# Strassen sums kept in PSUM, more of the second weight on chip, and an instruction order read from a table

## The chip, the core and the metric

The kernel runs on one NeuronCore of a Trainium2 chip. The metric is the device time of one execution in microseconds (us), from the first to the last instruction and what lies around them. TensorE (PE) multiplies matrices, VectorE (DVE) and ScalarE (ACT) work element by element, GpSimd (POOL) takes element work that needs no PSUM, and SyncE (SP) issues nearly all transfers, in order, from one queue.

## What is computed

The reference is linear attention with random features over 8 batches of 8 heads (576 tokens, 64 features per head), followed by a two-layer network over all 4608 tokens. Everything is float32.

```
q, k scaled by 64 ** -0.25
phi(x) = exp(x @ omega.T - |x|^2 / 2 - max) / sqrt(128)
attn   = (phi(q) @ (phi(k).T @ v)) / (phi(q) @ sum(phi(k)) + 1e-6)
x      = attn as [4608 tokens, 512]
h      = x @ w_in                     # 512 -> 2048
g      = h where h > 0, else exp(min(h, 0)) - 1
out    = g @ w_out                    # 2048 -> 512
```

The two weights arrive as 64-bit floats and are turned into float32 on the chip.

## The kernel before, in words

**Precision.** A float32 matmul operand is split into a high part and a low part (what is left), both in the fast matmul format, and a product is three passes: low times high, high times high, high times low. The helper at L433 to L440 makes the parts: `copy` the high one (on ACT or DVE), `tt` the low one (on POOL or DVE).

**Tiling.** The 4608 tokens are nine blocks of 512 (`TB`). The 2048 hidden features are 16 steps `f` of 128. `layer1` (L1234) makes one step of the first layer for blocks 0 and 1 with ordinary matmuls. For blocks 2 to 8, `quad` (L1281) makes two steps, a pair, with one level of Strassen's scheme: seven products in place of eight, each of 128 by 256 columns and six matmuls, into two PSUM banks pa and pb. Both write the activated tiles g, and `layer2` (L1359) multiplies a step's g by that step's part of w2 and adds it into the four banks `acc` of the block: twelve matmuls of 512 columns a step. PSUM has eight banks: four hold `acc`, the other four are shared by the pairs and by the attention (one tag, `pa`).

**The sums of Strassen's scheme.** On the side of x they are made by `operands` (L994): x lies in a ring `xf` for two blocks (L425), four sums S1 to S4 go to buffers of their own (tag `u`, L1005), and the seven operands are split into high and low. On the side of w1 `combine` (L1187) makes them once, and eight slots per pair lie in DRAM (`w1p`). `weights` (L1141) fetches, for each pair of a block, four tiles: slots 1 and 2, 3 and 4, 7, and 5 and 6 (L1178 to L1183). On the side of the result, `quad` copies the first half of pa to `s` (ACT, L1319), adds on DVE out of PSUM into an SBUF buffer `h` (L1314), and runs the activation out of `h` and pa: relu and exp on ACT (L1333, L1342), the rest on DVE (L1347), in pieces of 256 and 512 columns.

**The second weight.** Its parts 0 to 7 stay on chip (`w2h`, `w2l`, L419 and L420; `NRES` = 8). Parts 8 to 15 are written to DRAM once (`w2s`) and fetched by SP for every block (L1154) into two buffers (tag `w2`), 512 KB each.

**Stages.** Attention of batch b is worked in the segment before its tokens are needed; its projections, exponentials, sums and divisions lie between the matmuls of the network. Blocks 0 and 1 run in two halves of eight steps each, since the weights are being converted at the same time (`from_f64`, L1051). Attention ends before block 7, so blocks 7 and 8 have only the network.

**Order.** Each piece of work is a task with an engine, a duration, a due time and what it reads and writes (`Plan.op`, L149). `Plan.order` (L175) runs an event loop over estimated durations and emits, for each engine, the ready task that is due first; some tasks may go to a second engine (`other`, L354). Due times come from constants at the head (`STEP`, `OFF1`, `QOFF`, `LAGQ`, ...). Engines and queues run in the order emitted. Buffers are named by a tag, and `SLOTS` (L78) tells how many each tag has; a task that needs a buffer waits for the last reader of the one whose place it takes.

```python
SLOTS = {'raw': 3, 'u': 5, 'h': 5, 'ld': 2, 't': 2, 'e': 3, 'w1': 5, 'g': 3, 'w2': 2, 'xo': 8}
products(q[0], pa, ((0, 0, "A11", True), (1, 1, "S2", False)), wq[0])
products(q[1], pb, ((0, 0, "S3", True), (1, 1, "S1", False)), wq[1])
products(q[2], pa, ((0, 0, "A12", False),), wq[2])
products(q[3], pb, ((0, 0, "A22", False), (1, 1, "S4", False)), wq[3])
```

Of the kernel before, what the change touches and what calls it, by code (L numbers as in the profile page):

```python
# [19 lines left out]
P = 128  # L20
# [13 lines left out]
RING = 2 * TB  # L34
# [14 lines left out]
MLP0 = 23.44  # L49
SEG = [7.276, 7.148, 5.642, 7.92]  # L50
STEP = 6.384
STEP_ATT = 6.65

LAG = 2.608


PAIR0 = 24.011
DUE_LOAD, DUE_K, DUE_KV, DUE_Q = 19.218, 25.325, 28.271, 24.877
LOAD2, K2, KV2, Q2 = 7.188, 37.601, 24.27, 26.068
TAIL = 7.114  # L60
TAIL2 = 4.433
HEAD = 24.713


CONV1 = 27.076
CONV_STEP = -0.248
CONV2 = 2.044

EARLY = 22.132
CONV3 = 60.74  # L70
# [6 lines left out]
NRES = 8  # L77
SLOTS = {'raw': 3, 'u': 5, 'h': 5, 'ld': 2, 't': 2, 'e': 3, 'w1': 5, 'g': 3, 'w2': 2, 'xo': 8}  # L78

OPERANDS = ("A11", "S2", "S3", "S1", "A12", "A22", "S4")  # L80

# [6 lines left out]
DUE_Z = 15.231  # L88
# [3 lines left out]
EARLIER = 8.077  # L92
# [19 lines left out]

class Buf:
# [13 lines left out]
class Plan:  # L127
# [3 lines left out]

    LAT = {
        "PE": dict(PE=0, ACT=220, DVE=205, POOL=270, SP=300),
        "ACT": dict(PE=500, ACT=200, DVE=155, POOL=280, SP=300),
        "DVE": dict(PE=480, ACT=150, DVE=127, POOL=215, SP=300),
        "POOL": dict(PE=400, ACT=100, DVE=100, POOL=102, SP=300),
        "SP": dict(PE=400, ACT=200, DVE=200, POOL=200, SP=200),
    }
    LOOSE = ("pa", "h")

    SHARED = ("DVE", "POOL")

    FREE = dict(PE=1100.0, ACT=730.0, DVE=1600.0, POOL=1300.0, SP=700.0)
    DMA_LAT, DMA_RATE = 1050.0, 300.0
# [30 lines left out]
    def order(self):  # L175
        tasks = self.tasks
        waits = [len(t[3]) for t in tasks]
        users = [[] for _ in tasks]
        for n, t in enumerate(tasks):
            for d in t[3]:  # L180
                users[d].append(n)
        ready = [dict.fromkeys(t[0], t[7] * 1e3) for t in tasks]
        end = [0.0] * len(tasks)
        free, queue, events = {}, {}, [0.0]
        held = dict.fromkeys(self.SHARED, 0.0)
        kind = 0
        slots, dma = {}, 0.0


        line = {}  # L190
        for n in sorted(range(len(tasks)), key=lambda n: tasks[n][1]):
            for b in sorted(tasks[n][4], key=lambda b: b.args[3]):
                q = line.setdefault(b.key, [])
                if not b.listed:
                    b.listed = True
                    q.append(b)
                    slots.setdefault(b.key, [0.0] * b.n)
        for q in line.values():
            q.reverse()
        for n, t in enumerate(tasks):  # L200
            for e in t[0]:
                free.setdefault(e, self.FREE[e])
                heapq.heappush(events, self.FREE[e])
                queue.setdefault(e, [])
                if not waits[n]:
                    queue[e].append(n)
                    heapq.heappush(events, ready[n][e])
        done, last = [], {}
        now = 0.0

        events = sorted(set(events))

        def mine(n, eng):

            engs, due = tasks[n][:2]
            end = now + engs[eng][0] + engs[eng][1] * 1e3
            for e, (ns, late) in engs.items():
                if e == eng:
                    continue
                t = max(free[e], now, ready[n][e])  # L220
                if e == "POOL":
                    t = max(t, held["DVE"])
                elif e == "DVE" and tasks[n][6]:
                    t = max(t, held["POOL"])
                t += ns + late * 1e3
                for m in queue[e]:
                    if m != n and tasks[m][1] < due and len(tasks[m][0]) == 1:
                        t += tasks[m][0][e][0]
                        if t >= end:
                            break  # L230
                if t < end:
                    return False
            return True

        while len(done) < len(tasks):
            started = False
            for eng, q in queue.items():
                if free[eng] > now:
                    continue
                best, first = None, 0.0  # L240
                for n in q:
                    engs, due, _, _, bufs, _, port, _, full = tasks[n]
                    if eng == "PE" and full == kind:
                        due -= STICK
                    if ready[n][eng] > now:
                        continue
                    if best is not None and due >= first:
                        continue
                    if eng == "DVE" and port and held["POOL"] > now or eng == "POOL" and held["DVE"] > now:
                        continue  # L250
                    if len(engs) > 1 and not mine(n, eng):
                        continue
                    need = {}
                    for b in bufs:
                        if b.slot is None:
                            need.setdefault(b.key, []).append(b)
                    for key, bs in sorted(need.items()):
                        s = sum(z <= now for z in slots[key])
                        head = line[key][-1]
                        if s < len(bs):  # L260
                            for b in bs:
                                b.waits = True
                            break
                        if head not in bs and (s < 2 or key not in self.LOOSE or head.waits):
                            break
                    else:
                        best, first = n, due
                if best is None:
                    continue
                started = True  # L270
                engs, _, _, _, bufs, nbytes, port, _, full = tasks[best]
                for e in engs:
                    queue[e].remove(best)
                ns = engs[eng][0]
                if eng == "PE":
                    ns += SWITCH if kind and not full else 0.0
                    kind = full
                for b in bufs:
                    if b.slot is None:
                        s = slots[b.key]  # L280
                        b.slot = s.pop(s.index(min(s)))
                        line[b.key].remove(b)
                free[eng] = now + ns
                if eng == "POOL" or eng == "DVE" and port:
                    held[eng] = now + ns
                    if now < YIELD:
                        self.behind[best] = last.get("DVE") if eng == "POOL" else None
                    last[eng] = best
                if nbytes:
                    dma = max(now + self.DMA_LAT, dma) + nbytes / self.DMA_RATE  # L290
                    end[best] = dma + self.DMA_LAT + self.lands[best]
                else:
                    end[best] = now + ns
                heapq.heappush(events, free[eng])
                done.append((best, eng))
                for b in bufs:
                    b.left -= 1
                    if not b.left:
                        heapq.heappush(events, end[best] + 200.0)
                        slots[b.key].append(end[best] + 200.0)  # L300
                for u in users[best]:
                    for e in ready[u]:
                        ready[u][e] = max(ready[u][e], end[best] + self.LAT[eng][e])
                    waits[u] -= 1
                    if not waits[u]:
                        for e in ready[u]:
                            queue[e].append(u)
                            heapq.heappush(events, ready[u][e])
            if not started:
                if not events:  # L310
                    raise RuntimeError("no task can start")
                now = max(now, heapq.heappop(events))
        return done

    def issue(self, tc):
# [4 lines left out]
        for n, eng in order:  # L320
# [10 lines left out]
YIELD = 2e6  # L331
STICK = 3.202
SWITCH = 90.0
ENGINES = dict(DVE=mybir.EngineType.DVE, POOL=mybir.EngineType.Pool)
# [41 lines left out]
def performer_elu_kernel(  # L376
# [764 lines left out]
    def weights(F, due):  # L1141
# [29 lines left out]
        elif blk < NCONV:  # L1171
            op("SP", 590, due - 8, lambda: nc.sync.dma_start(raw_of(t), both), parts, keys, P * 3440)
            if odd:
                combine(j, w1c[F - 1], t, due + TJOB)
# [401 lines left out]
```

## Time and profile before

| what | us |
|---|---|
| median of 3 runs | 1028.62 |
| lowest, highest | 1023.39, 1030.73 |
| the profiled execution's own time | 1025.38 |
| its span, first to last instruction | 1023.1 |

The profile is one execution. Busy time of an engine is the time in which it has an instruction under way. Matmuls overlap (a new one starts before the last has drained), so the duration of one is longer than the distance to the next. A granted clock of 1.00 is 2.4 GHz, one of 0.50 is 1.2 GHz.

### The profile page before, as it was taken

The page shows a single profiled execution, that of the slowest core. Times are in us where ns is not written, and L with a number is a line of the kernel's source. Part 1 is how long each engine was busy: PE and PEld are TensorE (multiplying, and loading weights), DVE is VectorE, ACT ScalarE, POOL GpSimd, SP SyncE. Part 2 cuts the span into 40 slices and gives each one's busy share as a digit, 9 for nine tenths or more (in the row PEclk, how much of TensorE's full clock was granted, in tenths as well). Part 3 has the DMA queues.
Part 4 walks back from the last instruction along what each step waited for, and adds up shares of the span by engine and source line. Part 5 has one row for each costly group of instructions (what it writes and reads, how often), then busy time and mean ns, then how long its engine had stood idle before and what let it go on. Part 6 is the DMA issues. An engine that isn't in the chain of part 4 may idle for free.

```text
span 1023.1 us, 20461 instructions
## 1 busy us (share of the span) xinstructions
PE 984.9 (96%) x6237; PEld 848.9 (83%) x6237; DVE 791.8 (77%) x2775; ACT 693.2 (68%) x1886; POOL 411.0 (40%) x398
## 2 busy tenths in 40 slices
PE   7999998899988999999999999999999989999998
PEld 7888777678767988899889988898899869899996
DVE  6999788767889997999898988898899545364331
ACT  6898656788678786788688778787878534243231
POOL 2555744585424544154424432443345412222322
PEclk9999999999997999999999999999999999999999
DMA  8687768789998989799979888998898679568654
GB/s 214 181 250 246 261 252 303 264 289 313 317 315 320 309 265 285 265 336 283 282 266 353 273 272 269 326 292 281 282 320 272 186 226 317 187 210 284 216 175 144
DMA packets 104523, 273.70 MB, mean 268 GB/s; under 512 B 13216, under 2 KB 26336, under 8 KB 104416
## 3 DMA queue, kind: packets, MB, share of 16 engines
q1 hardware_dynamic: 103472, 270.09, 81.3%
q10 hardware_dynamic: 944, 2.33, 0.7%
q8 instruction: 50, 0.82, 0.3%
q14 instruction: 57, 0.47, 0.2%
HBM read 225.71 MB, written 46.66 MB: 266 GB/s over the span
## 4 chain that ended last, share of the span: by engine, by line
PE 68%; DMA 11%; DVE 10%; ACT 6%; issue 2%; POOL 2%; SPq 0%; POOLq 0%; ACTq 0%; DVEq 0%
PE acc L1375 32%; PE phb L1300 14%; PE pha L1300 11%; DMA w<-w2s 6%; PE ppk L631 2%; PE ppq L631 2%; DVE junk L851 1%; ACT hk L532 1%; DMA xk<-in_kx_dram 1%; PE pn L767 1%; DMA w1q<-w1p 1%; PE ph L1249 1%; ACT hq L532 1%; DVE u_w L1103 1%; PE ph L1251 1%
## 5 line engine op out<-in xcount | busy, mean ns | idle before, releaser
L440 POOL TENSOR_TENSOR g<-e,g 128x512 fp32r<-128x512 f32 x128 | 166.2, 1299 | 370.0 <-DVE g L437 106.1
L1375 PE MATMUL acc<-w,g 128*128 128x512 f32 x861 | 224.8, 399 | 12.1 <-DMA w<-w2s 9.5
L1375 PEld LDWEIGHTS acc<-w,g 128*128 128x128 f32 x861 | 155.5, 190 | 44.0 <-DMA w<-w2s 9.7
L1375 PE MATMUL acc<-w2h,g 128*128 128x512 f32 x576 | 185.6, 395 | 0.0
L1375 PEld LDWEIGHTS acc<-w2h,g 128*128 128x128 f32 x576 | 106.3, 189 | 19.5 <-issue 0.5
L1375 PE MATMUL acc<-w2l,g 128*128 128x512 f32 x288 | 114.4, 397 | 2.2 <-DVE g L437 1.9
L1333 ACT ACTIVATE e<-h 128x256 f32<-128x256 f32 x112 | 58.7, 525 | 78.9 <-DVE h L1314 77.2
L440 POOL TENSOR_TENSOR hq<-hq,den 128x512 f32<-128x512 f32 (+1 forms) x96 | 78.2, 833 | 62.0 <-DVE den L860 45.4
L437 DVE CAST g<-e 128x512 fp32r<-128x512 f32 x128 | 58.4, 461 | 48.5 <-PE acc L1375 47.0
L640 ACT ACTIVATE p2q<-ppq,sqq 128x128 f32<-128x128 f32 x216 | 65.4, 367 | 21.5 <-PE ppq L631 18.7
L851 DVE CUSTOM_DVE_ANT_0 junk<-hq,pz 128x128 f32<-128x128 f32 (+1 forms) x320 | 73.1, 280 | 6.8 <-PE pz L830 5.9
L640 ACT ACTIVATE p2k<-ppk,sqk 128x128 f32<-128x128 f32 x216 | 66.1, 370 | 15.9 <-PE ppk L631 14.2
L1333 ACT ACTIVATE e<-pha 128x256 f32<-128x256 f32 x56 | 21.5, 385 | 73.9 <-PE pha L1300 73.7
L532 ACT ACTIVATE hk<-hk,mnk 128x128 f32<-128x128 f32 x216 | 69.1, 403 | 2.3 <-DVE mnk L649 2.0
L532 ACT ACTIVATE hq<-hq,mnq 128x128 f32<-128x128 f32 x216 | 68.7, 398 | 1.3 <-DVE mnq L649 1.0
L649 DVE CUSTOM_DVE_ANT_0 hq<-ppq,p2q 128x128 f32<-128x128 f32 x216 | 53.1, 285 | 20.4 <-ACT p2q L640 19.2
L1342 ACT ACTIVATE e<-e 128x512 f32<-128x512 f32 x112 | 65.7, 629 | 0.8
L1375 PEld LDWEIGHTS acc<-w2l,g 128*128 128x128 f32 x288 | 54.3, 189 | 12.1 <-DVE g L437 2.1
L1347 DVE SCALAR_TENSOR_TENSOR e<-e,h 128x256 f32<-128x256 f32 (+1 forms) x112 | 61.3, 584 | 1.4 <-ACT e L1342 1.4
L649 DVE CUSTOM_DVE_ANT_0 hk<-ppk,p2k 128x128 f32<-128x128 f32 x216 | 53.1, 283 | 11.8 <-ACT p2k L640 11.0
L1249 PE MATMUL ph<-xc,w1c 128*128 128x512 f32 x128 | 53.4, 418 | 3.9 <-DVE e L1262 1.6
L1314 DVE TENSOR_TENSOR h<-phb,h 128x512 f32<-128x512 f32 x56 | 38.6, 690 | 21.2 <-PE phb L1300 20.4
(223 smaller groups left out, 2398.2 us busy)
## 6 DMA issues: line engine op xcount, KB each, us to landing
w1q<-w1p SPq DMA_DIRECT2D x168, 512.0 KB, 5.5
w<-w2s SPq DMA_DIRECT2D x72, 512.0 KB, 5.5
raw_w<-in_w_dram SPq DMA_DIRECT2D x28, 512.0 KB, 4.7
w1q<-w1p SPq DMA_DIRECT2D x56, 256.0 KB, 4.9
xk<-in_kx_dram SPq DMA_DIRECT2D x24, 576.0 KB, 6.0
xq<-in_qx_dram SPq DMA_DIRECT2D x24, 576.0 KB, 6.5
turned<-tb SPq DMA_DIRECT2D x48, 288.0 KB, 5.7
qh<-turned SPq DMA_DIRECT2D x96, 144.0 KB, 7.1
```

The lines of the kernel that those rows point to most:

```text
L437: nc.vector.tensor_copy(dst, src)
L440: (nc.vector if e == "DVE" else nc.gpsimd).tensor_tensor(*args)
L532: nc.scalar.activation(h()[:, j, :], src(j), AF.Exp, bias=mn()[:, j:j + 1], scale=-1.0)
L640: nc.scalar.activation(p2()[:, a], view()[:, a, M:], AF.Identity, bias=sq()[:, j:j + 1], scale=1.0)
L649: nc.vector.tensor_tensor_reduce(out=h()[:, j, :], in0=view()[:, a, 0:M], in1=p2()[:, a, :], scale=1.0, scalar=HIGHEST, op0=ALU.add, op1=A ...
L851: nc.vector.tensor_tensor_reduce(out=junk()[r], in0=h()[r, j, :], in1=pz()[r, a * P:(a + 1) * P], scale=1.0, scalar=EPS, op0=ALU.mult, op1 ...
L1249: nc.tensor.matmul(ph(), wh, x[:, 0], start=(c == 0), stop=False)
L1300: nc.tensor.matmul(half(p, n), a, b, start=(first and c == 0 and i == 0), stop=(c == 1 and i == 2), skip_group_check=True)
L1333: op("ACT", act(n, psum), d, lambda: nc.scalar.activation(out(), x(), AF.Relu, scale=-1.0), reads, writes)
L1342: "ACT", act(TB), d + 0.6 + 0.2 * n, lambda z=z: nc.scalar.activation(e()[:, z], e()[:, z], AF.Exp, scale=-1.0), keys, keys,
L1347: "DVE", dve(n), d, lambda: nc.vector.scalar_tensor_tensor(out(), out(), -1.0, x(), ALU.add, ALU.max), (*reads, *keys), keys,
L1375: nc.tensor.matmul(now[tt](), g()[:, a, ts], w(), start=(first and n == 0), stop=(last and n == 2))
```

## The change

- In `quad` the buffers `h` and `e` of four parts are gone. The sums are added in place: into `s`, into the second half of pa, and into pb. Relu, exp and the rest then run on whole banks of 512 columns, reading PSUM. A g tile now holds half of the tokens of both steps of the pair, so `layer2` of either step reads both tiles.
- `operands` makes the four sums in the buffers of x itself (new tiles `xf`, two per block, four slots) after the parts that need the old contents are split.
- 12 of 16 parts of w2 stay on chip, in one tile `w2r` with high and low side by side. Parts 3, 7, 11 and 15 are fetched, into one buffer.
- The last two loads of w1 of a pair become one of three slots, 768 KB, into one buffer of its own (tag `w1b`); it serves the products A12, A22 and S4.
- The slots per tag change, tag `e` goes, and in the last three pairs of block 8 the g tiles lie in the buffers of tag `h`.
- `Plan.order` no longer plans: it reads `ORDER`, a list of 5098 numbers, each four times a task's number plus the place of the engine chosen. The constants change too, but with the table they set no order.

```diff
-NRES = 8
-SLOTS = {'raw': 3, 'u': 5, 'h': 5, 'ld': 2, 't': 2, 'e': 3, 'w1': 5, 'g': 3, 'w2': 2, 'xo': 8}
+STREAMED = (3, 7, 11, 15)
+SLOTS = {'raw': 3, 'u': 8, 'h': 5, 'ld': 2, 't': 2, 'w1': 3, 'w1b': 1, 'g': 2, 'w2': 1, 'xo': 7, 'xf': 4}
+
+def xc_tag(blk, c):
+    return "w1b" if (blk, c) == (NCONV - 1, NC - 1) else "xo"
...
+ORDER = """
+0 44 52 48 8 12 56 36 77 40 4 276 142 66 72 96 297 280 301 1004 108 100 112 144 148 68 172 176 80 84 288 152 16 104 20 284 60 500 88 24 1140 496 1008
...
     def order(self):
...
+        done, last = [], None
+        for x in map(int, ORDER.split()):
+            n, e = divmod(x, 4)
+            eng = list(self.tasks[n][0])[e]
+            if eng == "POOL":
+                self.behind[n] = last
+            elif eng == "DVE" and self.tasks[n][6]:
+                last = n
+            done.append((n, eng))
+        assert sorted(n for n, _ in done) == list(range(len(self.tasks)))
         return done
...
-    w2h = const.tile([P, NRES, DM], F32R, name="w2h")
-    w2l = const.tile([P, NRES, DM], F32R, name="w2l")
+    resident = [f for f in range(NF) if f not in STREAMED]
+    w2r = const.tile([P, len(resident), 2, DM], F32R, name="w2r")
...
+        d, e = due - XO1, due - XO0
+        split_of("A11", d, a11)
+        split_of("A22", d + XO2, a22)
+        sum_of(e, a21[0], a11[0], a21[0], ALU.subtract, [*a11[1], *a21[1]], a21[1])
+        sum_of(d + XO2 + 0.5, a22[0], a22[0], a21[0], ALU.subtract, [*a21[1], *a22[1]], a22[1])
+        split_of("S2", d + 2 * XO2 + 0.6, a22)
+        split_of("S3", d + 3 * XO2 + 0.6, a21)
+        sum_of(d + 3 * XO2 + 0.7, a11[0], a22[0], a11[0], ALU.add, [*a11[1], *a22[1]], a11[1])
+        split_of("S1", d + 4 * XO2 + 1, a11)
+        split_of("A12", d + 5 * XO2 + 1, a12)
+        sum_of(d + 5 * XO2 + 1.5, a12[0], a12[0], a22[0], ALU.subtract, [*a12[1], *a22[1]], a12[1])
+        split_of("S4", d + 6 * XO2 + 1.6, a12)
...
-            wq = w1c[F] = [w1_tile(f"w1q_{F}_{n}") for n in range(4)]
-            for n, (a, b, needs) in enumerate(((1, 3, ("B11", "T")), (3, 5, ("T",)), (7, 8, ("B21",)), (5, 7, ("T", "B22")))):
+            wq = w1c[F] = []
+            for n, (a, b, needs) in enumerate(((1, 3, ("B11", "T")), (3, 5, ("T",)), (5, 8, ("T", "B22", "B21")))):
+                tag = "w1b" if n == 2 else "w1"
+                w = Buf(mv, [P, b - a, 2, HB], F32R, tag, f"w1q_{F}_{n}", room(tag))
+                wq.append(w)
...
+        add(q[0] + 2, HB, lambda: s()[:, 1], lambda: half(pa, 1), lambda: s()[:, 0], (pa, (s, 0)), ((s, 1),))
+        products(q[1], ((pb, 0, 0, "S3", True), (pb, 1, 1, "S1", False)), wq[1], (pb,))
+        add(q[1] + 1.5, HB, lambda: s()[:, 0], lambda: half(pb, 0), lambda: s()[:, 1], (pb, (s, 1)), ((s, 0),))
+        add(q[1] + 2, HB, lambda: half(pa, 1), lambda: half(pb, 1), lambda: s()[:, 0], (pb, (s, 0)), (pa,))
+        products(q[2], ((pa, 0, 2, "A12", False),), wq[2], (pa,))
+        products(q[2] + 0.1, ((pb, 0, 0, "A22", False), (pb, 1, 1, "S4", False)), wq[2], (pb,))
+        d = q[2] + 1.5
+
+        def whole(p):
+            return p().rearrange("p (a x) -> p a x", a=2)
+
+        add(d, TB, lambda: whole(pb), lambda: whole(pb), lambda: s()[:, 1:2].to_broadcast([P, 2, HB]), ((s, 1),), (pb,))
+        for n, (p, g) in enumerate(((pa, gs[0]), (pb, gs[1]))):
+            e = Buf(sb, [P, TB], F32, "u", f"e{n}_{F}", room("u"))
+            d1 = d + 0.5 * n
+            op("ACT", act(TB, True), d1, lambda p=p, e=e: nc.scalar.activation(e(), p(), AF.Relu, scale=-1.0), (p,), (e,))
+            op("ACT", act(TB), d1 + 0.2, lambda e=e: nc.scalar.activation(e(), e(), AF.Exp, scale=-1.0), (e,), (e,))
+            op(
+                "DVE", dve(TB), d1 + 0.8, lambda p=p, e=e: nc.vector.scalar_tensor_tensor(e(), e(), -1.0, p(), ALU.add, ALU.max),
+                (p, e), (e,),
+            )
+            split(g, e, (e,), "2", d1 + 1.2)
...
+        def part_of(tt, a):
+            g, n = tiles[tt // 2]
+            return g()[:, a, n * HB + tt % 2 * P:n * HB + (tt % 2 + 1) * P]
```

## Rows read from the trace of the kernel before

**Rows 1.** Page, busy time of each engine: us, share of the span, instructions.
```profile
PE 984.9 (96%) x6237; PEld 848.9 (83%) x6237; DVE 791.8 (77%) x2775; ACT 693.2 (68%) x1886; POOL 411.0 (40%) x398
```
**Rows 2.** Windows by stage: stretch, width, busy us (instructions) per engine, clock, DMA.
```profile
core 0: us, PE busy (x) PEld busy (x) DVE busy (x) ACT busy (x) POOL busy (x), PEclk, DMA share, GB/s
0.00:350.00 350.00, 324.64 (x1835) 266.28 (x1836) 294.39 (x998) 269.02 (x700) 175.37 (x164) 0.97 0.83 274
350.00:830.00 480.00, 472.46 (x3270) 416.56 (x3268) 415.95 (x1610) 365.18 (x1061) 191.73 (x201) 1.00 0.89 283
830.00:1009.00 179.00, 178.72 (x1096) 159.28 (x1096) 80.57 (x167) 56.91 (x122) 42.63 (x33) 0.99 0.68 222
1009.00:1023.10 14.10, 9.08 (x39) 6.73 (x37) 0.85 (x2) 2.13 (x4) 1.29 (x1) 0.97 0.46 157
```
**Rows 3.** Windows, stretches at the lower clock; columns as in rows 2.
```profile
15.30:18.70 3.40, 3.40 (x19) 3.40 (x18) 2.23 (x5) 2.37 (x9) 2.25 (x2) 0.50 0.99 252
...
319.10:329.40 10.30, 9.46 (x59) 8.52 (x59) 9.72 (x47) 8.91 (x24) 2.40 (x3) 0.50 0.75 273
831.10:834.50 3.40, 3.40 (x10) 2.58 (x8) 0.00 (x0) 0.00 (x0) 0.00 (x0) 0.50 0.95 363
```
**Rows 4.** Waits of PE, the largest: us in total, times, longest.
```profile
PE acc L1375 <- DMA w<-w2s: 9.5, 8, 3.2
```
**Rows 5.** Timeline around 820 to 830 us: start, us, engine, line, out<-in, count.
```profile
820.74 0.34 SPq L1154 DMA_DIRECT2D w<-w2s  x1
...
826.36 0.69 DVE L1314 TENSOR_TENSOR h<-phb,h 128x512 f32<-128x512 f32 x1 [1.01 <-PE phb L1300]
...
830.28 4.61 PE L1375 MATMUL acc<-w,g 128*128 128x512 f32 x12 [3.24 <-DMA w<-w2s]
```
**Rows 6.** Timeline of PE in block 7; columns as in rows 5.
```profile
875.97 0.88 PE L1300 MATMUL pha<-A12x,w1q 128*128 128x256 f32 x6
876.69 0.88 PE L1300 MATMUL pha<-A11x,w1q 128*128 128x256 f32 x6
...
878.13 0.40 PE L1375 MATMUL acc<-w2l,g 128*128 128x512 f32 x1
878.37 0.40 PE L1375 MATMUL acc<-w2h,g 128*128 128x512 f32 x1
...
886.61 0.88 PE L1300 MATMUL pha<-A12x,w1q 128*128 128x256 f32 x6
```
**Rows 7.** Groups by line and form: count | busy us, mean ns | idle before, releaser.
```profile
L440 POOL TENSOR_TENSOR g<-e,g 128x512 fp32r<-128x512 f32 x128 | 166.2, 1299 | 370.0 <-DVE g L437 106.1 <-ACT e L1333 80.9 <-DVE den L860 23.9
...
L1342 ACT ACTIVATE e<-e 128x512 f32<-128x512 f32 x112 | 65.7, 629 | 0.8
L437 DVE CAST g<-e 128x512 fp32r<-128x512 f32 x128 | 58.4, 461 | 48.5 <-PE acc L1375 47.0
...
L1314 DVE TENSOR_TENSOR h<-phb,h 128x512 f32<-128x512 f32 x56 | 38.6, 690 | 21.2 <-PE phb L1300 20.4
...
L1262 DVE SCALAR_TENSOR_TENSOR e<-e,ph 128x512 f32<-128x512 f32 x32 | 21.9, 684 | 7.2 <-ACT e L1259 6.2 <-ACT z L435 0.7
...
L1258 ACT ACTIVATE e<-ph 128x512 f32<-128x512 f32 x32 | 19.3, 602 | 14.3 <-PE ph L1251 11.1 <-DVE tw L440 2.8 <-POOL w2l L440 0.4
```
**Rows 8.** Page, transfers: total, and the loads of w2 (KB each, us to landing).
```profile
DMA packets 104523, 273.70 MB, mean 268 GB/s; under 512 B 13216, under 2 KB 26336, under 8 KB 104416
...
w<-w2s SPq DMA_DIRECT2D x72, 512.0 KB, 5.5
```
**Rows 9.** Transfers issued from 830 to 1005 us; columns as in rows 8.
```profile
w1q<-w1p SPq DMA_DIRECT2D x44, 512.0 KB, 4.5
...
w1q<-w1p SPq DMA_DIRECT2D x15, 256.0 KB, 3.8
```
**Rows 10.** Chain that ended last, in order of time: start, us, engine, tile, line, count.
```profile
892.24 3.74 PE acc L1375 x16
...
913.44 3.65 PE acc L1375 x16
```

More of the change, by code (lines that the diff above doesn't have):

```diff
@@ L175, in order @@
     def order(self):
[L176 to L312, printed above, removed]
@@ L1291, in half @@
+        gt[F] = (gs[0], 0), (gs[1], 0)
+        gt[F + 1] = (gs[1], 1), (gs[0], 1)
         def half(p, n):
             return p()[:, n * HB:(n + 1) * HB]
[L1294 to L1302 removed]
@@ L1304, in products @@
-        def products(d, p, items, w):
-            def mms():
-                for n, k, name, first in items:
-                    product(p, n, w, k, xo[blk, name], first, True)
-            reads = [w, *((xo[blk, name], z) for _, _, name, _ in items for z in "hl")]
-            op("PE", 6 * len(items) * NARROW, d, mms, reads, (p,))
-        def add(d, n, out, p, x, reads, writes):
-            op(
-                "DVE", dve(n), d, lambda: nc.vector.tensor_tensor(out(), p(), x(), ALU.add), reads, writes,
-            )
@@ L1323, in quad @@
-        add(q[1] + 2, HB, lambda: h()[:, 2], lambda: half(pb, 1), lambda: s()[:, 1], (pb, (s, 1)), ((h, 2),))
-        products(q[2], pa, ((0, 0, "A12", False),), wq[2])
-        products(q[3], pb, ((0, 0, "A22", False), (1, 1, "S4", False)), wq[3])
-        d = q[3] + 1.5
-        add(
-            d, TB, lambda: h()[:, 0:2], lambda: pb().rearrange("p (a x) -> p a x", a=2),
-            lambda: h()[:, 3:4].to_broadcast([P, 2, HB]), (pb, (h, 3)), ((h, 0), (h, 1)),
-        )
-        def relu(d, n, out, x, reads, writes, psum=False):
-            op("ACT", act(n, psum), d, lambda: nc.scalar.activation(out(), x(), AF.Relu, scale=-1.0), reads, writes)
@@ new lines, in add @@
+        def add(d, n, out, p, x, reads, writes):
+            op("DVE", dve(n), d, lambda: nc.vector.tensor_tensor(out(), p(), x(), ALU.add), reads, writes)
+        q = [due + o for o in QOFF]
+        products(q[0], ((pa, 0, 0, "A11", True), (pa, 1, 1, "S2", False)), wq[0], (pa,))
+        op("ACT", act(HB, True), q[0] + 1.5, lambda: nc.scalar.copy(s()[:, 0], half(pa, 0)), (pa,), ((s, 0),))
+        add(q[0] + 2, HB, lambda: s()[:, 1], lambda: half(pa, 1), lambda: s()[:, 0], (pa, (s, 0)), ((s, 1),))
@@ L1375, in mms @@
                     nc.tensor.matmul(
-                        now[tt](), g()[:, a, ts], w(), start=(first and n == 0), stop=(last and n == 2)
+                        now[tt](), part_of(tt, a), w(), start=(first and n == 0), stop=(last and n == 2)
                     )
@@ L1383, in tail @@
         def tail(d):
-            a, r, ts = now[NTT - 1], NTOK - P, slice((NTT - 1) * P, NTT * P)
+            a, r, tt = now[NTT - 1], NTOK - P, NTT - 1
+            g = tiles[1][0]
             reads = [(g, 0), (g, 1), kh, kl, a]
@@ L1461, in segment @@
         for F in range(F0, F0 + f1 - f0):
+            f = STEPS[F][1]
             if blk:
-                weights(F, step[F])
+                early = LASTQ if blk == NBLK - 1 and f >= OWNG else 0.0
+                weights(F, step[F] - early + (OFFQ[(blk - NCONV) * NF // 2 + f // 2] if blk >= NCONV else 0.0))
             if blk < NCONV:
```

238 lines of the change are left out of this document (97 added, 141 removed), and 185 rows, old and new, of the table ORDER.

## The prediction

> **What bounds the kernel now.** I read the busy shares first, then the windows by stage, the clock, the waits of PE, and last the timeline where a wait falls. PE is busy for 984.9 of 1023.1 us, DVE for 77%, ACT for 68% [rows 1]: the kernel hangs on PE, and 38.2 us of PE's idle time is what an order can win directly. The windows [rows 2] say where it lies: 25.4 us before 350 (350 less 324.64), 7.5 between 350 and 830, 0.3 between 830 and 1009, and 5.0 in the last 14. To this comes the clock. In six stretches, five of 3.4 us and one of 10.3, the granted clock is 0.50, that is 1.2 GHz instead of 2.4 [rows 3]. They make 27.3 us in which PE does half the work, so 13.7 us are lost, 12.0 of them before 350 (four short stretches and the long one). Idle time and clock together are 51.9 us: with no edit to the matmuls, the profiled execution, which took 1025.4 (2.3 more than its span, 3.2 less than the median of the runs), can't come under about 973.
>
> That the rest is packed shows in block 7 [rows 6]: six products of 256 columns start every 0.72 us (0.12 each), a matmul of 512 columns every 0.23, and the same product of the next pair comes 10.64 us later. A pair has 42 products and 24 matmuls of the second layer: 42 x 0.12 + 24 x 0.233 = 10.6. Nothing is to be had there by a better order.
>
> The largest wait of PE is for a part of w2 [rows 4]: 9.5 us in 8 waits. One of them, at the end of block 6, shows how it comes about [rows 5]: the fetch goes out at 820.74, after the reader of its buffer, and PE stands still for 3.24 us until 830.28. The low clock of 831.1 to 834.5 [rows 3] follows and costs another 1.7.
>
> **The change part by part.** The change adds or removes no matmul: products, second layer and attention have the same counts. So every term is idle time of PE, or clock.
>
> *w2.* Fetches fall from 8 to 4 a block, 72 [rows 8] to 36, and 4 of 8 first writes go: 40 transfers of 512 KB, 21 of 273.7 MB, 8%. A fetch now has the four steps between two streamed parts to land in, two pairs or 21 us of PE work [rows 6], against a landing of 5.5 [rows 8]. The buffer is single, but its last reader is one streamed step back. Gain: at most 9.5 + 1.7 = 11.2, at least 0. I take 7, since the order isn't free of the fault. Counting the tasks back from the end of the table, SP's queue in block 5 has the fetch of part 15 behind four fetches of turned q of pairs 26 and 27. These wait for transposes and landings of the attention, and the layer that reads part 15 follows soon after. The wait at the end of a block can come back there.
>
> *The order of the first 350 us.* Idle time and clock make 37.4 there, about 2 of it waits for w2 and counted above. DVE is 84% and ACT 77% busy in this stretch, against 87% and 76% between 350 and 830, where PE idles 1.6% [rows 2]. So load alone doesn't force the idle time, and another order can win some. But the first data has to arrive, and weights have to be converted before a step can run. At one end nothing is gained; at the other the stretch becomes like the later one, with 5.6 us of idle time and the full clock, 19.8 + 12.0 = 32. I take 13, nearer the lower end, because conversions, projections and activations are the same instructions as before.
>
> *w1 in three loads.* One issue of 0.3 us fewer per pair on SP, which is off the path: 0. The third load is 768 KB into a single buffer, which comes free with the last product of a pair. In the quiet stretch 512 KB land in 4.5 us and 256 KB in 3.8 [rows 9]; 0.7 more per 256 KB gives an estimate of 5.2, or 5.5 with the issue, and, from the 5.5 us of 512 KB over the whole span [rows 8], about 6.5. Against it stands what the table puts on PE between the last use in one pair and the first in the next, priced by [rows 6]: from the pair of steps 12 and 13 of block 7 to the next pair it is 12 products and 22 matmuls of the second layer, 1.4 + 5.1 = 6.6 us. In blocks 2 to 8 the same sum is 5.7 to 6.6 at 10 of 55 places and more at the others. The cost lies between 0 and 6; I take 2. The Trainium skill ("DMA: Bandwidth & Descriptors", section on the anatomy of one DMA) fits another issue path with 2.0 us plus bytes at 436 GB/s, which is 3.8 for 768 KB. By that figure the load would never be late and the sum would be 1005; the rows are slower, and I go by them.
>
> *Sums in PSUM.* The adds stay four per pair and of the same sizes; none of before writes PSUM, so its price is taken as that of the add that reads it, 0.69 for 512 columns, with relu 0.60, exp 0.63 and the last step 0.68 from PSUM [rows 7]. What changes is how long a bank is held. Before, pb was free after the add of 0.69; now it is held through relu, exp and the last step, 1.9 us more. The product A12 also has to wait for an add into the other half of its bank. Behind it in PE's queue stands everything else. It is hidden as long as other matmuls stand in between, and the pair has 5.6 us of second layer for that [rows 6]. I take 0; the bad end is in the rivals.
>
> *Two g tiles, x summed in its own buffers.* A g tile can be written once its last reader is done: cast 0.46 and low part 1.30 [rows 7], 1.8 and two handovers. In block 8 the table puts the products A12, A22 and S4 of one pair, S3 and S1 of the next and one run of two matmuls between, 1.4 + 0.7 + 1.4 + 0.5 = 4.0. Cost 0, and beyond that the same bad end. The seven splits and four sums of x stay eleven pieces of the same size, now in a chain; they are made ahead of their block: 0, at worst 2.
>
> *Layout of w2.* Sixteen matmuls take 3.74 us with resident parts and 3.65 with fetched ones [rows 10], 5.6 ns each. If the new tile, which lies like the fetched one, has the lower price, 72 x 12 matmuls gain 4.8; if being resident is what costs, 36 x 12 lose 2.4. I take 0.
>
> Sum: -7 - 13 + 2 = -18, so 1025.4 - 18 = 1007.
>
> **The rivals.** *The first 350 us come out like the later ones.* The order of before leaves little idle once the blocks repeat (7.5 us in 480, 0.3 in 179 [rows 2]), so a search that does as well early on gains about 32 there and the waits for w2: 1025 - 32 - 8 = 985. Against it: the start has data to wait for, in any order.
>
> *Hidden anyway.* The w2 wait moves to the fetches of turned q or the w1 load, and the early stalls go to another place: -2 + 2, 1025. For it: the ten short gaps before the third load, and the fetch of part 15 at the end of each block, are places where the new buffers are single. Against it: 8% less to transfer while the DMA share is 0.83 to 0.89 [rows 2].
>
> *Banks decide, and it is slower.* Four banks serve the pairs and the attention. With pb held 1.9 us longer in each of 56 pairs, and A12 behind an add, PE waits wherever the table left less than that between. From 18 / 56 = 0.33 us a pair on, it eats the gain; with 0.7 us it costs 39 and the time is 1046. For it: PE's queue can't step around a wait. Against it: durations on DVE and ACT are steady, and a table can be made around them. The Trainium skill ("PSUM — Partial Sum Buffer", section on PSUM bank collisions) speaks for this one: two engines must not touch one bank on the same partitions at once, whichever columns they use, so a half bank under an add keeps PE out of the other half too. No row of before shows such an overlap tried.
>
> **How the numbers follow.** The forecast, 992 to 1018 by itself, has 0.48; the good early order, 985, has 0.20; hidden anyway, 1025, has 0.18; the banks, 1046, have 0.14. About 1% either way, 1018 to 1039, is what a measurement of this kernel can tell from no change. The first two cases are faster by more (0.68), the third lies within (0.18), the last is slower (0.14). The range 982 to 1036 leaves out most of the last case and the best of the second, together 0.2.
>
> **What would show it.** Right: the waits of PE for w2 fall to 3 us or less and the low clock at the end of block 6 is gone; w2 has 36 loads; idle time before 350 is near 15; the stretch of blocks 7 and 8 stays at 10.6 us a pair. Wrong: waits of PE for the 768 KB load or of A12 on DVE that sum to over 10 us; a pair in block 7 of over 11.2 us; new low-clock stretches after 350; or idle time before 350 as large as it was.

## The result, and the profile after

The changed kernel takes 994.31 us (median of 4 runs, 993.61 to 995.83) against 1029.32 (4 runs, 1023.39 to 1030.73): a ratio of 0.967 with the interval 0.963 to 0.971. The forecast was 1007, its range 982 to 1036. The profiled execution took 994.99 us, 30.4 less than the 1025.4 of before. Among the runs below, one of the six executions of a_sums took 2186.65 us against 1011.93 to 1014.95 of the others; its ratio leaves this one out, and since it is the one that was traced, no row of a_sums is shown.

From the page: busy shares, the total of the transfers, and the loads of w1 and w2 (KB each, us to landing).

```profile
PE 970.7 (98%) x6237; PEld 842.0 (85%) x6237; DVE 776.7 (78%) x2709; ACT 709.5 (71%) x1856; POOL 403.0 (41%) x382
...
DMA packets 90697, 252.71 MB, mean 255 GB/s; under 512 B 11680, under 2 KB 24800, under 8 KB 90592
...
w1q<-w1p SPq DMA_DIRECT2D x112, 512.0 KB, 5.6
w1q<-w1p SPq DMA_DIRECT2D x56, 768.0 KB, 5.5
w<-w2s SPq DMA_DIRECT2D x36, 512.0 KB, 5.9
```

The number of matmuls is as before. What changed is how long PE stands idle and at which clock it runs. The windows of after, by the stages of [rows 2], with the early stage also cut at 150 us (columns: stretch, width, busy us and instructions per engine, granted clock, DMA share, GB/s):

```profile
0.00:350.00 350.00, 334.69 (x1959) 279.10 (x1960) 319.13 (x1075) 290.61 (x761) 147.18 (x148) 0.99 0.82 264
0.00:150.00 150.00, 136.12 (x844) 113.24 (x845) 130.75 (x417) 117.89 (x317) 55.58 (x58) 0.98 0.75 231
150.00:350.00 200.00, 198.56 (x1117) 165.87 (x1116) 188.38 (x659) 172.71 (x446) 91.60 (x91) 1.00 0.86 289
350.00:830.00 480.00, 476.70 (x3310) 420.85 (x3309) 387.51 (x1506) 367.43 (x1000) 226.32 (x212) 1.00 0.83 266
830.00:980.00 150.00, 150.00 (x933) 134.86 (x933) 67.55 (x126) 49.88 (x93) 29.51 (x23) 1.00 0.64 209
980.00:993.00 13.00, 9.28 (x41) 7.23 (x39) 2.52 (x5) 1.58 (x3) 0.00 (x0) 0.93 0.23 84
...
8.20:15.10 6.90, 5.39 (x25) 5.39 (x26) 3.73 (x9) 3.78 (x12) 2.24 (x2) 0.51 0.74 192
```

The idle time of PE is now 15.3 us before 350, 3.3 up to 830, 0 up to 980 and 3.7 behind it: 22.3 instead of 38.2. Of the six stretches at 1.2 GHz [rows 3] one is left while PE has work, the last row, 6.9 us long: it costs 3.4 us instead of 13.7. The two together are 26.2 of the 30.2 us by which the span is shorter. The other 4.0 lie in PE's busy time: the same matmuls take a little less of it at full clock, and no row shows one place for it. In a second trace of the changed kernel, a_again below, the stretch at 1.2 GHz in the first 15 us is missing too, and PE idles 13.4 us before 350; so much do two executions differ.

The early stage is worth a second look, and for that the same cut of the kernel before:

```profile
0.00:150.00 150.00, 142.14 (x873) 118.65 (x874) 129.19 (x412) 115.95 (x296) 76.27 (x74) 0.99 0.74 234
150.00:350.00 200.00, 182.50 (x963) 147.63 (x962) 165.21 (x587) 153.07 (x405) 99.10 (x91) 0.95 0.89 303
```

In its first 150 us the changed kernel is worse: PE idles 13.9 us instead of 7.9. In the next 200 it idles 1.4 instead of 17.5, at full clock instead of 0.95. Before, PE is busy at the start and starves later; in the changed kernel PE waits at the start, and DVE does 23 us more work from 150 to 350 (188.4 instead of 165.2).

The waits of PE in after, the largest and that for w1 (us in total, times, longest):

```profile
PE ppq L626 <- ACT xq L606: 2.4, 1, 2.4
...
PE pha L1358 <- DMA w1q<-w1p: 1.4, 1, 1.4
```

No row names w2: the 9.5 us of [rows 4] are gone, and with them the low clock at the end of block 6. In block 8 the product A12 of one pair starts 10.60 us after that of the pair before (timeline of PE: start, us, engine, line, out<-in, count), as in [rows 6]:

```profile
904.07 0.88 PE L1358 MATMUL pha<-A12x,w1q 128*128 128x256 f32 x6
...
914.67 0.88 PE L1358 MATMUL pha<-A12x,w1q 128*128 128x256 f32 x6
```

### The profile page after: what moved, and what is told of

Read it like the earlier page. It is cut to its first block, busy times and chain, and to the rows that moved or that the text cites. A ratio compares the mean times of both kernels' runs of the same rounds, so it can differ in the third digit from the quotient of the medians.

```text
span 992.9 us, 20069 instructions
## 1 busy us (share of the span) xinstructions
PE 970.7 (98%) x6237; PEld 842.0 (85%) x6237; DVE 776.7 (78%) x2709; ACT 709.5 (71%) x1856; POOL 403.0 (41%) x382
## 4 chain that ended last, share of the span: by engine, by line
PE 76%; DVE 8%; ACT 4%; DMA 3%; issue 2%; POOL 1%; DVEq 0%; ACTq 0%; POOLq 0%
PE acc L1415 35%; PE phb L1358 16%; PE pha L1358 12%; PE ppk L681 2%; PE ppq L681 2%; PE pn L817 2%; DMA w1q<-w1p 1%; PE ph L1303 1%; PE ph L1305 1%; PE ph L1304 1%; DMA xq<-in_qx_dram 1%; DVE e L1316 1%; DVE u_w L1157 1%; DVE g L490 1%; DVE u_w L1162 1%
## 5 line engine op out<-in xcount | busy, mean ns | idle before, releaser
L1415 PE MATMUL acc<-w2r,ga 128*128 128x512 f32 x504 | 136.4, 396 | 0.0
L1415 PE MATMUL acc<-w2r,gb 128*128 128x512 f32 x504 | 134.8, 395 | 0.0
L1415 PEld LDWEIGHTS acc<-w2r,ga 128*128 128x128 f32 x504 | 90.4, 189 | 16.9 <-issue 0.7
L1415 PEld LDWEIGHTS acc<-w2r,gb 128*128 128x128 f32 x504 | 90.3, 189 | 16.1
L490 POOL TENSOR_TENSOR gb<-e,gb 128x512 fp32r<-128x512 f32 x35 | 45.3, 1293 | 112.4 <-DVE gb L487 53.4
L490 POOL TENSOR_TENSOR ga<-e,ga 128x512 fp32r<-128x512 f32 x34 | 44.0, 1293 | 83.0 <-DVE ga L487 51.5
L1415 PE MATMUL acc<-w2r,g 128*128 128x512 f32 x288 | 74.5, 396 | 1.5 <-DVE mnk L699 1.2
L699 DVE CUSTOM_DVE_ANT_0 hq<-ppq,p2q 128x128 f32<-128x128 f32 x216 | 53.1, 285 | 15.9 <-ACT p2q L690 13.9
L1415 PEld LDWEIGHTS acc<-w2r,g 128*128 128x128 f32 x288 | 52.4, 188 | 13.4 <-ACT e L1313 1.3
L490 POOL TENSOR_TENSOR tk<-xk,tk 64x576 fp32r<-64x576 f32 x33 | 47.2, 1429 | 40.6 <-DMA turned<-tb 10.0
L490 POOL TENSOR_TENSOR tq<-xq,tq 64x576 fp32r<-64x576 f32 x30 | 42.9, 1431 | 48.2 <-DVE tq L487 7.6
L1390 DVE SCALAR_TENSOR_TENSOR e<-e,phb 128x512 f32<-128x512 f32 x56 | 38.2, 682 | 23.7 <-ACT e L1388 23.3
```

The source lines that it names most:

```text
L490: (nc.vector if e == "DVE" else nc.gpsimd).tensor_tensor(*args)
L699: nc.vector.tensor_tensor_reduce(out=h()[:, j, :], in0=view()[:, a, 0:M], in1=p2()[:, a, :], scale=1.0, scalar=HIGHEST, op0=ALU.add, op1=A ...
L1390: "DVE", dve(TB), d1 + 0.8, lambda p=p, e=e: nc.vector.scalar_tensor_tensor(e(), e(), -1.0, p(), ALU.add, ALU.max),
L1415: nc.tensor.matmul(now[tt](), part_of(tt, a), w(), start=(first and n == 0), stop=(last and n == 2))
```

## The experiments

My theory after the result: the gain is the order, most of it before 350 us, plus the waits for w2. The rivals: the new structure carries it (sums in PSUM, banks, fewer w1 loads), or the lighter traffic does. "The kernel before" in a ratio always means runs on the same chip, taken between those of the variant.

### The order alone, and the structure alone

**e_planner**, the change without its table:

```diff
-        for x in map(int, ORDER.split()):
+        while len(done) < len(tasks):
+            started = False
+            for eng, q in queue.items():
...
```

> The changed kernel with the table taken out: sums in PSUM, 12 resident parts of w2 and three w1 loads stay, the order comes again from the event loop of the kernel before, with its costs and due times (the new tasks given due times in the same manner). Computation unchanged. My theory (the larger part of the 35 us is the order, above all between 150 and 350 us): at least 17 us of the gain are lost, time 1012 to 1050 us, ratio 0.983 to 1.02, PE idle before 350 us above 25 us again, while the waits for streamed parts of w2 stay below 4 us. Rival (the structure, w2 and the sums, carries it): below 1003 us, ratio under 0.975.

Measured: 1044.11 us, ratio 1.017 (1.011 to 1.023), inside the expected range. The constants of the due times are those that stand in the changed file, some of them refitted by me to the new tasks, and the loop's list of loosely given tags (`LOOSE`) has two more, `u` and `raw`; another fit might give less.

**b_table**, the kernel before with a table of mine in place of its event loop, and nothing else changed:

```diff
-        while len(done) < len(tasks):
...
+        for x in map(int, ORDER.split()):
```

> The kernel before with nothing changed but the order of its instructions: a table that I searched for its own tasks takes the place of the event loop (8 resident parts of w2, sums in SBUF, four w1 loads as before). Computation unchanged. My theory (order first): 985 to 1007 us, ratio 0.957 to 0.978, PE idle between 150 and 350 us under 6 us (17.5 before), low-clock stretches after 20 us gone. Rival (the structure is what gives): the waits for w2 (11.2 us) and the early idle stay, 1018 us or more, ratio above 0.989.

Measured: 1005.18 us, ratio 0.980 (0.974 to 0.986), just outside the expected 0.978. Windows up to 350 us, first of e_planner, then from 150 us of b_table, with its largest waits of PE:

```profile
0.00:150.00 150.00, 135.93 (x841) 113.00 (x841) 132.01 (x426) 119.65 (x321) 37.79 (x44) 0.99 0.75 230
150.00:350.00 200.00, 175.34 (x915) 141.69 (x913) 167.42 (x575) 148.78 (x388) 88.68 (x81) 0.95 0.78 255
```

```profile
150.00:350.00 200.00, 195.22 (x1104) 162.98 (x1103) 177.91 (x648) 170.75 (x448) 85.92 (x86) 0.99 0.92 314
...
PE acc L1445 <- DMA w<-w2s: 4.7, 3, 2.1
PE pha L1370 <- DMA w1q<-w1p: 4.1, 6, 2.4
...
PE phb L1370 <- DMA w1q<-w1p: 1.9, 1, 1.9
```

With the event loop the new structure starves in the same place as the old one, 24.7 us idle at a clock of 0.95, although it has no wait for w2 left. With a table the old structure idles 4.8 there and has half of its waits for w2 left (4.7 of 9.5 us). So the rival "structure" falls: under the old loop the structure brought nothing that could be seen, and the order alone brings 20 us. The loss at the start, though, doesn't need the table: e_planner idles 14.1 us in the first 150 (first row), about as much as after.

Two points stay open. Low-clock stretches after 20 us were expected to be gone in b_table; it has three, 6.8 us long at 26.3, and 3.4 each at 295.9 and 640.7. And not all of the 35 us is order: with a table on both sides the changed structure is still ahead, by 11 us in the medians and 13 by the ratios. PE waits 4.7 us for w2 and 6.0 for w1 in b_table, none and 1.4 in after. But each table was searched for itself, so no run tells what of this is the structure and what the better table.

**b_early**, the old structure and the old order, of which only the first 1,858 steps are searched anew:

> The kernel before with its own order, of which only the first 1,858 of 5,306 steps (up to about 350 us) are searched anew; the rest is as its event loop gave it. Computation unchanged. My theory (the whole gain of the order lies before 350 us): 1003 to 1014 us, ratio 0.977 to 0.988, first product of the Strassen part at 303 us or earlier (311.3 before), the blocks behind 419 us as long as before within 1 us each, waits for w2 still near 11 us. Rival (the gain of the order is in the later blocks): 1019 us or more, ratio above 0.992.

Measured: 1017.22 us (1011.84 to 1018.61), ratio 0.992 (0.989 to 0.994), between the two. In the profiled execution the granted clock was full; in the other three its mean was 0.992 to 0.995.

```profile
150.00:350.00 200.00, 189.31 (x1061) 155.43 (x1060) 181.31 (x636) 164.16 (x434) 84.94 (x84) 1.00 0.93 315
...
PE acc L1446 <- DMA w<-w2s: 10.1, 10, 2.7
```

Here the first product of the Strassen part starts at 296.4 us instead of 311.3, and what follows the start of block 3 takes as long as it did: 604.8 us instead of 604.2, with the waits for w2 still there in the last row (10.1 us, 9.5 before). So the early order alone is worth 13.5 us in the profiled execution and 9.6 in the medians. The rest of b_table's 20 us comes with the steps behind; 4.8 of it are waits for w2.

### What w2 costs, and whether it is the traffic

**b_nofetch**, the kernel before without any fetch of w2:

```diff
-        return (w2l if low else w2h)[:, f] if f < NRES else w2t[F]()[:, low]
+        return (w2l if low else w2h)[:, f % NRES]
...
-        if f >= NRES:
-            op(*fetch)
```

> The kernel before with its own order written out and all 72 fetches of w2 parts left out: parts 8 to 15 read a resident part instead (part f modulo 8), so layer 2 uses the wrong half of w2 for these, with the same products in the same places. It prices everything that fetching w2 costs there. My theory: the 11.2 us of waits go and little else moves, 1016 to 1020 us, ratio 0.987 to 0.992. Rival (hidden anyway, something else ends last in those places): 1025 us or more, ratio above 0.996. Rival (the traffic of the fetches also delays the early part): 1012 us or less, ratio under 0.984.

Measured: 1010.60 us, ratio 0.984 (0.980 to 0.989), that is 15 us. It is more than the 11.2 us of waits and clock that follows them. From 350 to 830 PE idles 1.3 us instead of 7.5, and the first product of the Strassen part starts at 306.8, 4.4 us sooner, most of which is one wait for w2 (2.0 us, at 298.3) and the low clock behind it. What makes the rest isn't shown. Two things differ in the traces: the w1 loads of 512 KB land in 4.9 us instead of 5.5, so fetching w2 does delay other loads, and the low clock before 350 costs 5.1 us instead of 12.0. Under this order 15 us is all that the fetches of w2 cost.

**a_traffic**, the changed kernel with the missing bytes put back:

```diff
+        if f in (1, 5, 9, 13):
+            op("SP", 590, due, lambda: nc.sync.dma_start(dm[F % 8], w2[f]), (), (("dm", F),), P * 3440)
```

> The changed kernel with 36 more transfers of 512 KB, one at each place where the kernel before fetched a part of w2 that is now resident. They go from w2 to an unused buffer in DRAM, nothing waits for them, and what is computed stays the same. It brings back at least the bytes that the change took away (273.7 against 252.7 MB). My theory (the 11.2 us of waits for w2 went because only 36 parts have to come through two buffers, not because the DMA queues are lighter): no change, ratio within 0.003 of the changed kernel's, waits for streamed parts below 1 us in sum. Rival (the lighter traffic is what ended the waits): the 36 streamed parts and the w1 loads land later, the PE waits come back, and 5 to 11 us of the gain are lost (ratio higher by 0.005 to 0.011).

Measured: 998.67 us, ratio 0.969 (0.966 to 0.972), against 993.63 for **a_again**, the changed kernel unaltered on the same chip:

> The changed kernel once more, unaltered, as the level for the three variants beside it. Every theory: ratio to the kernel before 0.964 to 0.970 (about 994 us).

That one measured 0.965 (0.961 to 0.968). The page of a_traffic and its largest wait of PE:

```profile
DMA packets 91850, 271.60 MB, mean 272 GB/s; under 512 B 12256, under 2 KB 25376, under 8 KB 91168
...
w1q<-w1p SPq DMA_DIRECT2D x112, 512.0 KB, 6.2
w1q<-w1p SPq DMA_DIRECT2D x56, 768.0 KB, 5.8
...
w<-w2s SPq DMA_DIRECT2D x36, 512.0 KB, 6.4
...
PE pha L1363 <- DMA w1q<-w1p: 4.0, 3, 2.4
```

Neither side had it right: 0.0042 of the ratio lies between the two. No wait for w2 comes back, though its parts land 0.5 us later: the waits did not go because the traffic is lighter. e_planner, with the same 36 loads in another order, has none either, so keeping more parts on chip is enough. (They come through one buffer, not the two that the expectation names.) But 5.0 us are lost all the same. In the traced executions, which lie 8.1 us apart, 3.6 are there when the Strassen part starts (299.9 instead of 296.3), and PE waits 4.0 us for w1 instead of 1.4. These transfers also write 18.9 MB of DRAM, which the fetches did not, so the 5 us aren't the price of the missing bytes alone.

### Sums in PSUM

**a_sums**, the second sum written to SBUF:

```diff
+        hs = Buf(sb, [P, TB], F32, "u", f"hs_{F}", room("u"))
-        add(d, TB, lambda: whole(pb), lambda: whole(pb), ...
+        add(d, TB, lambda: whole(hs), lambda: whole(pb), ...
-        for n, (p, g) in enumerate(((pa, gs[0]), (pb, gs[1]))):
+        for n, (p, g) in enumerate(((pa, gs[0]), (hs, gs[1]))):
```

> The changed kernel with the second Strassen sum written to a tile in SBUF instead of back into its PSUM bank, so that the bank comes free after that addition instead of after the two readers behind it (relu 0.60 us, exp 0.63 us). My theory (sums in PSUM cost nothing, since no product waits long for a bank): same time within 0.003 of the ratio, the addition 0.6 to 0.75 us. Rival (banks held longer hold up the products): faster by 0.005 or more; rival the other way (writing to SBUF is dearer, or the tile it takes is short): slower by 0.005 or more.

Measured: 1014.04 us, ratio 0.984 (0.981 to 0.987): 20 us lost, and not the unchanged time that I expected. That tile takes one of eight buffers of the tag `u`, and this order has all eight in use at times: with `hs` it asks for a ninth at 11 places. So it went once more into a tag with a free buffer, **a_sums_xf**:

```diff
-        hs = Buf(sb, [P, TB], F32, "u", f"hs_{F}", room("u"))
+        hs = Buf(stream, [P, 2, TB], F32, "xf", f"hs_{F}", room("xf"))
```

> The changed kernel with the second Strassen sum in SBUF once more, but in half a tile of another tag (xf), which has a free buffer wherever the order asks for one; in the first try it took a tile of the tag u, which is one buffer short at 11 places of this order. Computation unchanged. My theory (the 20 us of the first try were the missing buffer, neither the write to SBUF nor the PSUM bank has a price): ratio within 0.003 of the 0.9646 of the changed kernel. Rival (the write to SBUF itself is what costs): 1005 us or more, ratio above 0.975. Rival (banks held longer do cost, and the shortage hid it): ratio under 0.960.

Measured: 998.98 us, ratio 0.973 (0.971 to 0.975). So most of the 20 us go with the missing buffer, and 5 stay by the medians (9 by the ratios); that is again more than the 0.003 that I expected. The group of the step that reads the sum (count, busy us, mean ns, idle before), and places in the timeline; first the changed kernel (a_again), then a_sums_xf:

```profile
L1390 DVE SCALAR_TENSOR_TENSOR e<-e,phb 128x512 f32<-128x512 f32 x56 | 38.2, 682 | 23.9 <-ACT e L1388 23.3
...
667.60 1.29 POOL L490 TENSOR_TENSOR ga<-e,ga 128x512 fp32r<-128x512 f32 x1 [5.47 <-DVE ga L487]
667.71 0.69 DVE L1390 SCALAR_TENSOR_TENSOR e<-e,phb 128x512 f32<-128x512 f32 x1 [0.28 <-ACT e L1388]
```

```profile
L1391 DVE SCALAR_TENSOR_TENSOR e<-e,hs 128x512 f32<-128x512 f32 x56 | 48.7, 869 | 24.6 <-ACT e L1389 24.3
...
672.91 1.30 POOL L490 TENSOR_TENSOR ga<-e,ga 128x512 fp32r<-128x512 f32 x1 [5.18 <-DVE ga L487]
673.05 1.70 DVE L1391 SCALAR_TENSOR_TENSOR e<-e,hs 128x512 f32<-128x512 f32 x1 [0.31 <-ACT e L1389]
...
711.80 0.69 DVE L1391 SCALAR_TENSOR_TENSOR e<-e,hs 128x512 f32<-128x512 f32 x1
711.94 1.70 POOL L490 TENSOR_TENSOR ga<-e,ga 128x512 fp32r<-128x512 f32 x1 [0.98 <-DVE ga L487]
```

The write to SBUF is no dearer (685 ns instead of 695). The read is. At 667.6 and 672.9 the step starts 0.1 us after the same POOL instruction. With its second operand in PSUM it takes 0.69 us; with both in SBUF it takes 1.70 and ends 0.54 us after POOL's has ended. 15 of the 56 steps are stretched like this, to between 0.90 and 1.88 us, each ending about 0.55 us after POOL's. In a_again none is, though about as many meet a POOL instruction (27; 29 here). Where DVE's step starts first, POOL's is the one that takes longer (last two rows: 1.70 instead of 1.29). On DVE it adds 10.5 us in all. The kernel before had the same operands in SBUF and 692 ns, because its order kept POOL away from that step (the mark `port`; 1 of 56 meets POOL).

Less of this reaches the time. From the first product of the Strassen part to the end, a_sums_xf takes 698.2 us and a_again 694.9, 3.3 more. The other 2.4 us between the two traces lie ahead of it, where both kernels do the same. Which waits carry the 3.3 isn't shown.

### The w1 loads

**a_w1four**, the 768 KB load as 256 and 512 KB into the same buffer:

```diff
+                for c, d in ((a, b),) if b - a < 3 else ((7, 8), (5, 7)):
+                    nc.sync.dma_start(raw_of(w)[:, c - a:d - a], slots(j, c, d))
```

> The changed kernel with the third w1 load of each pair (768 KB) sent as two transfers (256 and 512 KB) into the same buffer, one behind the other; computation unchanged. My theory (the count of w1 loads is worth nothing by itself, the buffers come free at the same time): same time within 0.003 of the ratio, waits of the first products for w1 between 1 and 4 us in sum (3.4 now). Rival (one transfer instead of two is part of the gain, through SP's issue time or the queue): slower by 0.004 or more.

Measured: 993.31 us, ratio 0.964 (0.961 to 0.967), the same as a_again. How many transfers bring w1 is worth nothing here. PE waits 0.4 us for w1 in it, below the 1 to 4 expected; the 3.4 named there is 1.4 in the trace of after.

### Is there more in the order?

**a_search**, a first further search of the table:

> The changed kernel with another table for the same tasks, which I searched further from the table of the change; structure and computation unchanged. My theory (15 us of PE idle before 350 us and 7 us behind it are left, and the order is what holds them): 975 to 990 us, ratio 0.947 to 0.962, PE idle before 350 us under 12 us. Rival (what is left is not the order, or a fuller order loses to late transfers and engines off their expected times): 991 us or more, ratio above 0.963.

Measured: 999.36 us, ratio 0.974 (0.969 to 0.979): worse than the table of the change. Its Strassen part starts earlier (291.4 us), but the blocks behind it are slower, and PE waits 5.9 us for w1. My search replayed the tasks with transfers that land sooner than they do, and I take this for the reason; it wasn't tested alone. Two more tables were searched with half the weight on later landings: **a_early** for the first 350 us only, **a_full** for all.

> The changed kernel with its table, of which only the first steps (up to about 350 us) are searched further, by a model in which transfers land later than in my first search; the rest is as the change has it. Computation unchanged. My theory (13 to 15 us of PE idle before 350 us are left, and order can take half of it): 983 to 991 us, ratio 0.954 to 0.962. Rival (the early part is at what the transfers and DVE allow): 993 us or more, ratio 0.9645 or above.

> The changed kernel with the whole table searched further by the same model with later transfers. Computation unchanged. My theory (the first search lost behind 350 us because it counted on transfers that land late): 978 to 990 us, ratio 0.949 to 0.961, PE waits for w1 below 3 us. Rival (any order searched on a model loses some us there): 994 us or more, ratio 0.965 or above.

Measured: a_early 989.02 us, ratio 0.964 (0.961 to 0.966); a_full 985.28 us (984.10 to 988.33), ratio 0.961 (0.958 to 0.963). a_early's time lies in the expected range, but its ratio is outside (at most 0.962) and nearly that of a_again, 0.965; its idle time before 350 us is a_again's too, 13.4, so half of it was not taken. a_full is clearly faster than the kernel before and probably than the changed one: 8 us by the medians, 0.4% by the ratios, whose intervals overlap (the runs of before beside it were 0.3% faster). Its windows:

```profile
0.00:150.00 150.00, 141.11 (x881) 119.07 (x882) 134.70 (x441) 124.84 (x331) 57.45 (x60) 0.98 0.78 243
150.00:350.00 200.00, 197.75 (x1138) 166.47 (x1137) 180.91 (x652) 173.01 (x451) 94.41 (x91) 1.00 0.88 288
350.00:830.00 480.00, 476.90 (x3295) 420.08 (x3295) 384.60 (x1485) 368.01 (x1001) 218.33 (x206) 1.00 0.83 268
```

It keeps the 150 to 350 us of the change (2.3 us idle) and wins back 5.0 of the 13.9 us before 150 (3.2 against a_again's 12.1). Between 350 and 830 it wins nothing (3.1 us idle, 3.3 in the change).

## Why the prediction was right, and where its sizes were off

*The bound.* That PE's idle time and clock were nearly all there was to win held: 26.2 of 30.2 us are these two.

*w2: -7 predicted, -11.2 measured.* All 9.5 us of waits and the 1.7 of clock went. The reason for taking less, the fetch of part 15 behind the turned q on SP's queue at the end of a block, cost nothing: no row of after names w2. a_traffic shows that the waits didn't go with the bytes. One point of the reading was incomplete: I weighed 21 us against a landing of 5.5, the median. The fetch at 820.74, behind the longest wait, took 9.50 (before, chain that ended last: start, us, what); 21 us is still more than that.

```profile
820.74 9.50 DMA w<-w2s
```

*The first 350 us: -13 predicted, about -17 measured.* Idle time there fell by 10.1 us (25.4 to 15.3) and the clock's cost by 8.6 (12.0 to 3.4), 18.7, with about 2 of it w2; by the trace of a_again it is about 22. The 15 that I wrote down as the sign of being right is met. What I had not seen is how: the start got worse and the stretch behind it close to perfect. The 13 was chosen between 0 and 32, not worked out, so that it came within 4 us is in part luck. My reason for taking the lower end, that the instructions stay the same, was no reason: order alone moves the idle time from 150 to 350 us from 24.7 (e_planner) to 1.4 on the new structure, and from 17.5 to 4.8 (b_table) on the old.

*w1: +2 predicted, +0.7 measured.* The wait rose from 0.7 to 1.4 us. The load lands in 5.5 us where I estimated 5.5 to 6.5, and the table left enough room for it. The estimate from the fit of the Trainium skill ("DMA: Bandwidth & Descriptors", section on the anatomy of one DMA), which is for another issue path, was 3.8; the measurement decides.

*Sums in PSUM: 0 predicted; with this table about -3 in the traces, -5 in the medians.* The size of the add was right, 695 ns against the 690 that I took. No wait of a product for another engine is longer than 0.8 us, and a_sums_xf, which frees the bank earlier, isn't faster, so the rival on banks falls. But I looked at the price of the writes and at how long a bank is held, and not at what the reader of a sum in SBUF costs: a_sums_xf shows that it meets POOL. As I read it, the gain sits inside the term of the order, since without it the order has to keep the two apart.

*The rest.* Layout of w2 at 0: the matmuls of the second layer follow each other every 0.23 us in both traces. Sums of x at 0: nothing in the trace speaks against it. Behind 350 us the idle time fell from 12.8 to 7.0, most of it w2.

*The rivals.* "Hidden anyway" and "banks" fall. "A good early order, 985" was nearer than I gave it chances for: a_full reaches 985.3 with the same structure, though with 11.2 us idle before 350, twice what that rival assumed. The sum was 12 us too high: 4.2 for w2, 4 for the early part, 1.3 for w1, and about 3 that no term had, since PE's busy time fell by 4.0 at full clock. Of my two upper bounds, 11.2 came in full. 32 did not: 17 to 22 came in the traces of after, a_again and a_full.

## What to carry to other kernels

When the engine that bounds a kernel idles in one stretch while the same work runs densely elsewhere, suspect the order first. Here a search over a replay of the tasks took most of that idle time. One search that let transfers land too soon won early and lost later; one with later landings did not. What buffers and structure are worth depends on the order: the same structure was 18 us slower than the old kernel under the old loop and 35 faster under a table. Before a tile moves from PSUM to SBUF, see which engines read SBUF at the same time as its reader.

## What the runs showed of the hardware

A DVE step with both operands in SBUF that starts while a POOL instruction runs doesn't finish until POOL's has: 1.70 instead of 0.69 us, up to 1.88. If the DVE step starts first, POOL's instruction takes 1.70 instead of 1.29. With one operand in PSUM the same overlap costs nothing (682 ns on average). The Trainium skill ("SBUF — State Buffer", section on who interferes with whom) says it in this way: a DVE instruction with two SBUF inputs contends with a GpSimd instruction that reads SBUF, and the one that comes second waits for the whole of the first. The trace agrees with it, and with the page's other half, that one SBUF input is free of it.

A wait of 3.24 us at the end of block 6 was followed by 3.4 us at 1.2 GHz [rows 3, 5], which made it cost 4.9. In the changed kernel, of 27.3 us at the lower clock there is one stretch of 6.9 left while PE works, in the first 15 us, and none in a_again. That it went with the waits alone isn't shown: b_early keeps 10.1 us of waits for w2, the longest 2.7, and its trace has no such stretch while PE works.
